# Held weight loads, and reciprocals and small layernorm terms on ScalarE, in a fused attention and gated-MLP block

## The chip, the cores and the metric

The kernel runs on one core of a Trainium2 chip. The metric is the device time in microseconds, taken as the median of several runs; the profile shows one execution. The engines are named as the profile names them: PE (TensorE, matmuls), PEld (its weight loads), DVE (VectorE), ACT (ScalarE), POOL (GpSimd) and SP (SyncE, from whose queue every DMA of this kernel is issued). L12 means line 12 of the kernel before.

## The reference

The block is linear attention followed by a gated MLP, each with a layernorm in front and a residual around it, on x of shape 1 x 2048 x 1024 in bf16:

```python
def _A_ref(x, wqkv, wo):
    B, S, D = x.shape
    H = 32; Dh = D // H
    qkv = (lambda x, *d: x.transpose(*d))((x @ wqkv).reshape(B, S, 3, H, Dh), 2, 0, 3, 1, 4)
    q, k, v = qkv[0], qkv[1], qkv[2]
    phi = lambda t: jnp.where(t > 0, t + 1, jnp.exp(t)) + 1e-6
    pq, pk = phi(q), phi(k)
    kv = jnp.einsum("bhsd,bhse->bhde", pk, v)
    z = jnp.einsum("bhsd->bhd", pk)
    num = jnp.einsum("bhqd,bhde->bhqe", pq, kv)
    den = jnp.einsum("bhqd,bhd->bhq", pq, z)[..., None] + 1e-6
    o = num / den
    return (lambda x, *d: x.transpose(*d))(o, 0, 2, 1, 3).reshape(B, S, D) @ wo

def _B_ref(x, W_gate, W_up, W_down):
    gate = jnp.einsum("bsd,df->bsf", x, W_gate)
    up = jnp.einsum("bsd,df->bsf", x, W_up)
    gate = gate * (lambda x, dt: x.astype(dt))(gate > 0, gate.dtype)
    h = gate * up
    return jnp.einsum("bsf,fd->bsd", h, W_down)

x = A_x
h = x + _A_ref(_layernorm(x, axis=-1), A_wqkv, A_wo)
h2 = h + _B_ref(_layernorm(h, axis=-1), B_W_gate, B_W_up, B_W_down)
```

F, the width of the MLP, is 3584.

## The kernel before

The large products are done with Strassen's scheme (seven products of half-size blocks in place of eight), so each needs sums of blocks of its left and right operands, which DVE makes. The 2048 tokens are 16 tiles of 128.

The work goes through these stages:

- *K and V* (0 to 124.7 us in the profile). `ln_T` loads a tile of x, normalises it and transposes it into xT. Tiles are taken in four units of four; `k_unit` and `v_unit` make K (with phi applied, tile pk, which lies in wo_mem) and V, and `kv_tile` adds up kv and z. The weight sums of Q (`q_sums`, L127 to L130 on tiles wq_sb and tq) stand at the end of this stage in the code, but run as soon as DVE's order allows. Q's weights wq_sb are loaded with two DMAs of 1 MB (L372), written in the code after unit 0.
- *Q of the first half* (124.7 to about 149 us): `q_unit(0, c)` writes phi(Q) into pqT.
- *Attention, steps 0 to 7* (to about 203 us). For each of the 16 token tiles there are five stages, begun at a lag of 0, 1, 1, 2 and 4 steps: `nd` (num and den by matmuls, L473, in three pieces of 3, 3 and 2 chunks, each in one PSUM bank; den on ACT, L477; its reciprocal on DVE, L479; the product o_sb on DVE, L480), `oT` (a transposing DMA, L487), `x_in` (a load of the residual, L491), `wo_h` (the product with wo, L500; the residual and row sums, L502; a store of h, L505; the layernorm, L510 to L516) and `hn_T` (a transposing DMA, L519). The matmuls of Q's second half, `rest`, are dealt out over these eight steps.
- *Attention, steps 8 to 19* (to 299 us). The first four feature chunks of the MLP's first token half fill PE between the steps (`begin`, `narrow`, L612). Their weights come from `load_group` of groups 0 and 1, the early loads: wg and wu, each in two halves of 512 KB (L453), eight DMAs in all, written in the code before step 0 and all issued in one go. Their sums are L559 to L562.
- *The rest of the MLP* (299 to 768.6 us): gate and up by `quad_steps`, with each further weight group loaded as it is reached, then the product with W_down (`down`).

The PSUM pool of tag "ab" has three banks. `nd` takes three of them in a step and `wo_h` two, so attn's matmuls wait until o_sb has been made out of a bank. o_sb has two buffers.

Each engine and the queue of SP run their instructions in order; the framework places the instructions by its own estimate of when each is ready, with earlier code first, and adds the waits. The tile pool of wg and wu reuses memory of the Q stage, so the early loads wait for the last phi of Q's first half (L191 on DVE, just before 153 us).

Of the kernel before, what the change touches and what calls it, by code (L numbers as in the profile page):

```python
# [7 lines left out]
ACT = mybir.ActivationFunctionType  # L8
ALU = mybir.AluOpType
# [22 lines left out]
def block_kernel(ctx: ExitStack, tc: tile.TileContext, x, wqkv, wo, wg, wu, wd, out, H: int):  # L32
    nc = tc.nc
# [87 lines left out]
    def right_ops(w, t):  # L121

        (b11, b12), (b21, b22) = [[w[:, k * KH:(k + 1) * KH, j * NW:(j + 1) * NW] for j in range(2)] for k in range(2)]
        t1, t2, t4, t3 = t[:, 0], t[:, 1], t[:, 2], b12.bitcast(FP16)

        def sums():
            nc.vector.tensor_tensor(out=t1, in0=b12, in1=b11, op=ALU.subtract)  # L127
            nc.vector.tensor_tensor(out=t2, in0=b22, in1=t1, op=ALU.subtract)
            nc.vector.tensor_tensor(out=t3, in0=b22, in1=b12, op=ALU.subtract)
            nc.vector.tensor_tensor(out=t4, in0=b21, in1=t2, op=ALU.subtract)  # L130

        return (b11, b21, b22, t4, t1, t2, t3), sums

    def strassen(pool, work, mm, fin, sbufs=3):

# [65 lines left out]
    with ExitStack() as actx:  # L201
# [16 lines left out]
        def load_w(dst, j, col):  # L218
            nc.sync.dma_start(out=dst[:, :, j * NW:(j + 1) * NW], in_=wqkv_v[:, :, col + j * NW:col + (j + 1) * NW])
# [144 lines left out]
        for n, t in enumerate(units[0]):  # L364
# [3 lines left out]
            if n == 1:  # L368
                sums_unit(1)
                k_sums()  # L370
        for j in range(2):
            load_w(wq_sb, j, 0)  # L372
        for u in range(1, NU):
            todo = atiles[4 * u + 4:4 * u + 8]
            for _ in k_unit(u):
                if todo:
                    ln_T(todo.pop(0))
            if u == 1:
                v_sums()
            for t in units[u - 1]:  # L380
                kv_tile(t)
            new_v(u)
            for n, _ in enumerate(v_unit(u)):
                if n == 1 and u + 1 < NU:
                    sums_unit(u + 1)
# [60 lines left out]
    wu_v = wu.rearrange("(kc p) (h f) -> p kc h f", p=P, h=2)  # L446

    def load_group(g):
        tiles = []
        for nm, v in (("wg", wg_v), ("wu", wu_v)):  # L450
            w_sb = wpool.tile([P, KC, 2, GP * P], BF16, tag=nm, name=nm)
            for h in range(2):
                nc.sync.dma_start(out=w_sb[:, :, h, :], in_=v[:, :, h, g * GP * P:(g + 1) * GP * P])  # L453
            tiles.append(w_sb)
        return tiles

    early = [load_group(g) for g in range(NE // GP)]
    pieces = [(c, min(GPB, KC - c)) for c in range(0, KC, GPB)]

    def attn_stages(t):  # L460

# [4 lines left out]
        def nd():  # L466
            o_sb = bwork.tile([P, D], BF16, tag="o_sb", name="o_sb")
            st["o"] = o_sb
            ov = o_sb[:].rearrange("p (k h e) -> p k h e", k=KC, h=HPC)
            for c0, n in pieces:  # L470
                ps = ndpool.tile([P, NW], FP32, tag="ab", name="nd")
                for c in range(c0, c0 + n):
                    nc.tensor.matmul(ps[:, (c - c0) * NDW:(c - c0 + 1) * NDW], lhsT=pqT[:, c, t * P:(t + 1) * P],  # L473
                                     rhs=kvz[:, c, :], start=True, stop=True)
                ndv = ps[:, 0:n * NDW].rearrange("p (k w) -> p k w", w=NDW)
                den = bsmall.tile([P, GPB, HPC], FP32, tag="den", name="den")
                nc.scalar.activation(out=den[:, 0:n], in_=ndv[:, :, P:NDW], func=ACT.Identity, bias=deps[:], scale=1.0)  # L477
                rd = bsmall.tile([P, GPB, HPC], FP32, tag="rd", name="rd")
                nc.vector.reciprocal(out=rd[:, 0:n], in_=den[:, 0:n])  # L479
                nc.vector.tensor_tensor(  # L480
                    out=ov[:, c0:c0 + n], in0=ndv[:, :, 0:P].rearrange("p k (h e) -> p k h e", h=HPC),
                    in1=rd[:, 0:n, :].unsqueeze(3).to_broadcast([P, n, HPC, Dh]), op=ALU.mult)
# [11 lines left out]
        def wo_h():  # L494
# [12 lines left out]

            sm = bsmall.tile([P, 6], FP32, tag="sm", name="sm")
            nmean, var, lnv, rstd, nmr = (sm[:, i:i + 1] for i in range(5))
            nc.vector.tensor_tensor(out=nmean, in0=tot[:, 0:1], in1=tot[:, 1:2], op=ALU.add)  # L510
            nc.vector.tensor_scalar(out=nmean, in0=nmean, scalar1=-1.0 / D, scalar2=None, op0=ALU.mult)
            nc.scalar.activation(out=st["hn"][:], in_=h_sb[:], func=ACT.Square, bias=nmean, scale=1.0, accum_out=var)
            nc.scalar.activation(out=lnv, in_=var, func=ACT.Ln, bias=LN_EPS, scale=1.0 / D)
            nc.scalar.activation(out=rstd, in_=lnv, func=ACT.Exp, scale=-0.5)
            nc.vector.tensor_tensor(out=nmr, in0=nmean, in1=rstd, op=ALU.mult)
            nc.scalar.activation(out=st["hn"][:], in_=h_sb[:], func=ACT.Identity, bias=nmr, scale=rstd)  # L516

        def hn_T():
# [19 lines left out]
    rest = [p for s in range(1, NS) for c in range(0, KH, 2) for p in [q_unit(s, c)] * 6]  # L538
    for step in range(QSTEPS):
        attn_step(step)  # L540
        for p in rest[step * len(rest) // QSTEPS:(step + 1) * len(rest) // QSTEPS]:
            next(p)
    q1ctx.close()
# [153 lines left out]
    for n, items in enumerate(todo):  # L697
# [2 lines left out]
            for q in range(4):  # L700
                nc.sync.dma_start(out=hh0[q][:, 0:NE, :], in_=hh_dram[0][q][:, 0:NE, :])
        if n >= NE:
            wt = load_group(items[0][2])
            w = {fi: sums(wt, fi) for fi in range(GP)}
        if n == len(todo) - 1:
            first_wd = load_wd(0, 0, 0, prepool)
# [163 lines left out]
```

## Time and profile before

| what | value |
|---|---|
| median of 7 runs | 772.88 us (770.54 to 775.36) |
| the profiled execution | 770.78 us |
| its span in the profile | 768.6 us |
| mean granted clock of PE | 0.998 |
| PE busy, 0 to 20 us | 11.19 us |
| PE busy, 20 to 60 us | 37.75 us of 40 |
| PE busy, 124.7 to 148.9 us | 24.09 us of 24.2 |
| PE busy, 299 to 595.1 us | 291.51 us of 296.1 |
| PE busy, 595.1 to 768.6 us | 169.07 us of 173.5 |
| early weight loads (wg, wu), issue to landing | 5.4 and 5.5 us, median of all |
| wq_sb loads, issue to landing | 11.4 us, median of two |
| oT and hn transposes, issue to landing | 3.1 and 3.5 us, median |

The page gives busy time for each engine, and the windows give the same for chosen stretches. Busy times of neighbouring instructions on one engine overlap a little. In a line of the timeline, the bracket at the end tells how long the engine had been idle before the instruction and what released it. A wait for several things is put down to the one that came last.

In the K and V stage DVE has been the fuller engine from 20 to 60 us (38.75 of 40), with the DMA engines full up to about 26 us. The four sums of Q's weights run on DVE at 64.1, 65.8, 67.0 and 69.9 us, each 1.21 us, though the first matmul that needs wq_sb starts at 124.7 us. The page's DMA part lists SP as the issuer of every transfer: 89.15 MB through one hardware queue.

### The profile page before, as it was taken

What the parts mean: (1) busy time and instruction counts of PE and PEld (TensorE: products, weight loads), DVE (VectorE), ACT (ScalarE), POOL (GpSimd) and SP (SyncE); (2) the same over time, 40 slices, a digit from 0 to 9 for tenths busy, and PEclk for the clock granted to TensorE, in tenths of its full rate; (3) what the DMA queues carried; (4) which work ended last, traced back from release to release, by engine and by line L of the source; (5) the groups of instructions that cost most, each with busy time, mean ns of one, the idle gap of its engine ahead of it and who ended that gap; (6) DMA issues with size and microseconds to landing.
All of it is one profiled execution on the core that took longest, in us unless ns stands there. A gap on an engine that the chain in (4) does not pass through costs nothing.

```text
span 768.6 us, 9558 instructions
## 1 busy us (share of the span) xinstructions
PE 736.5 (96%) x3524; PEld 339.2 (44%) x3584; DVE 488.9 (64%) x948; ACT 313.6 (41%) x529; POOL 3.8 (0%) x34
## 2 busy tenths in 40 slices
PE   5989999989889999999999999999998999999998
PEld 2444555434444444444444444444443444444443
DVE  5999454877897776656374554746545891349632
ACT  4876554866757554444444444444444000000000
POOL 0000000000000000000000000000000000000000
PEclk9999999999999999999999999999999999999999
DMA  9961003095786526154023140140001986971001
GB/s 320 255 137 41 1 1 110 1 246 137 177 173 166 135 76 195 60 158 130 7 73 86 34 130 8 41 118 28 29 7 46 332 263 205 314 270 49 28 27 55
DMA packets 125150, 89.76 MB, mean 117 GB/s; under 512 B 50352, under 2 KB 116912, under 8 KB 124592
## 3 DMA queue, kind: packets, MB, share of 16 engines
q1 hardware_dynamic: 125104, 89.15, 40.8%
q8 instruction: 28, 0.46, 0.2%
q14 instruction: 18, 0.15, 0.1%
HBM read 59.77 MB, written 17.83 MB: 101 GB/s over the span
## 4 chain that ended last, share of the span: by engine, by line
PE 49%; DVE 13%; ACT 4%; issue 3%; DMA 3%; DVEq 0%; SPq 0%; ACTq 0%
PE A L579 15%; PE accA L740 10%; PE E L579 8%; PE accE L740 6%; DVE gu L598 4%; PE Dp L579 3%; PE attn L500 2%; ACT snap L593 2%; DMA hn<-hn 2%; PE accD L740 2%; PE Aq L612 1%; DVE hh L601 1%; DMA out_dram<-o 1%; ACT gu L600 1%; DVE x_res L502 1%
## 5 line engine op out<-in xcount | busy, mean ns | idle before, releaser
L598 DVE TENSOR_TENSOR gu<-E,snap 128x1024 bf16<-128x1024 f32 x48 | 58.6, 1222 | 90.1 <-ACT snap L593 87.5
L593 ACT COPY snap<-A 128x1024 f32<-128x1024 f32 x72 | 72.1, 1008 | 84.0 <-PE A L579 84.0
L740 PEld LDWEIGHTS <-hh 128*128 128x128 bf16 (+1 forms) x560 | 54.7, 98 | 67.6 <-DVE gu L598 1.8
L600 ACT ACTIVATE gu<-gu 128x512 bf16<-128x512 bf16 x72 | 45.4, 630 | 86.2 <-DVE gu L598 85.9
L740 PE MATMUL accA<-wd,hh 128*128 128x512 f16 (+1 forms) x333 | 73.2, 379 | 1.5 <-DVE gu L598 1.3
L500 PE MATMUL attn<-wo_mem,oT 128*128 128x512 bf16 x250 | 58.8, 385 | 8.3 <-DMA oT<-o_sb 3.4
L579 PEld LDWEIGHTS <-tg 128*128 128x128 f16 x384 | 37.5, 98 | 49.5 <-issue 5.7
L579 PEld LDWEIGHTS <-tu 128*128 128x128 f16 x384 | 37.5, 98 | 45.4
L601 DVE TENSOR_TENSOR hh<-gu 128x512 bf16<-128x512 bf16 x72 | 30.4, 422 | 38.4 <-ACT gu L600 38.4
L579 PE MATMUL A<-hn,tg 128*128 128x512 f16 (+1 forms) x191 | 49.2, 379 | 1.2 <-ACT snap L593 1.1
L579 PE MATMUL A<-hn,tu 128*128 128x512 f16 (+1 forms) x192 | 49.3, 379 | 0.0
L143 ACT COPY u<-Aq 128x512 f32<-128x512 f32 x56 | 32.1, 582 | 40.4 <-PE Aq L276 20.3
L579 PEld LDWEIGHTS <-wg 128*128 128x128 bf16 x288 | 28.1, 98 | 34.5 <-issue 1.1
L579 PEld LDWEIGHTS <-wu 128*128 128x128 bf16 x288 | 28.2, 98 | 34.0
L500 PEld LDWEIGHTS <-oT 128*128 128x128 bf16 x256 | 24.4, 99 | 40.8 <-issue 10.5
L740 PEld LDWEIGHTS <-s 128*128 128x128 f16 x224 | 21.9, 98 | 27.2 <-issue 0.8
L598 DVE TENSOR_TENSOR gu<-Dp,snap 128x1024 bf16<-128x1024 f32 x24 | 29.3, 1219 | 2.3 <-PE Dp L579 2.3
L276 PEld LDWEIGHTS <-xT 128*128 128x128 bf16 (+1 forms) x192 | 18.6, 98 | 23.1 <-issue 1.5
L748 DVE TENSOR_TENSOR u<-accA,hres 128x512 f32<-128x512 f32 x16 | 10.7, 686 | 28.2 <-PE accA L740 27.6
L189 ACT ACTIVATE e<-pq_mem,negb 128x512 bf16<-128x512 bf16 x32 | 22.7, 720 | 10.6 <-DVE pq_mem L184 10.5
L502 DVE SCALAR_TENSOR_TENSOR x_res<-attn,x_res 128x512 bf16<-128x512 f32 x32 | 21.9, 686 | 7.9 <-PE attn L500 7.9
L480 DVE TENSOR_TENSOR o_sb<-nd,rd 128x384 bf16<-128x384 f32 (+1 forms) x48 | 23.1, 508 | 4.0 <-DMA oT<-o_sb 3.2
(159 smaller groups left out, 1207.2 us busy)
## 6 DMA issues: line engine op xcount, KB each, us to landing
wd<-in_B_W_down_dram SPq DMA_DIRECT2D x16, 896.0 KB, 6.9
hh_dram<-hh SPq DMA_DIRECT2D x72, 128.0 KB, 1.7
wg<-in_B_W_gate_dram SPq DMA_DIRECT2D x14, 512.0 KB, 5.4
wu<-in_B_W_up_dram SPq DMA_DIRECT2D x14, 512.0 KB, 5.5
hh<-hh_dram SPq DMA_DIRECT2D x4, 1792.0 KB, 8.3
x_sb<-in_A_x_dram SPq DMA_DIRECT2D x16, 256.0 KB, 3.8
x_res<-in_A_x_dram SPq DMA_DIRECT2D x16, 256.0 KB, 3.0
h_dram<-x_res SPq DMA_DIRECT2D x16, 256.0 KB, 2.6
```

What stands on the lines that cost most here:

```text
L143: nc.scalar.copy(out=snaps[nm, v], in_=A[v][:])
L189: nc.scalar.activation(out=e, in_=dst, func=ACT.Exp, bias=negb[:, 0:1], scale=1.0)
L276: nc.tensor.matmul(ps[:], lhsT=left[m - 1][:, kc, r + v * P:r + (v + 1) * P], rhs=right[m - 1][:, kc, :], start=(start and kc == 0), stop= ...
L480: nc.vector.tensor_tensor(out=ov[:, c0:c0 + n], in0=ndv[:, :, 0:P].rearrange("p k (h e) -> p k h e", h=HPC), in1=rd[:, 0:n, :].unsqueeze(3 ...
L500: nc.tensor.matmul(ps[:], lhsT=st["oT"][:, c, :], rhs=wo_sb[:, c, j * NW:(j + 1) * NW], start=(c == 0), stop=(c == KC - 1))
L502: nc.vector.scalar_tensor_tensor(out=h_sb[:, j * NW:(j + 1) * NW], in0=ps[:], scalar=1.0, in1=h_sb[:, j * NW:(j + 1) * NW], op0=ALU.mult, ...
L579: nc.tensor.matmul(ps[:, v, :], lhsT=w[v][m - 1][:, kc, :], rhs=left[m - 1][:, kc, :], start=(start and kc == 0), stop=(kc == KH - 1), ski ...
L593: nc.scalar.copy(out=m[:], in_=ps[:])
L598: nc.vector.tensor_tensor(out=gu[:], in0=ps[:], in1=m[:], op=ALU.add)
L600: nc.scalar.activation(out=gu[:, 0, :], in_=gu[:, 0, :], func=ACT.Relu)
L601: nc.vector.tensor_tensor(out=d, in0=gu[:, 0, :], in1=gu[:, 1, :], op=ALU.mult)
L740: nc.tensor.matmul(accs[tt][:], lhsT=lhs[:, half * FD + f, tt * P:(tt + 1) * P], rhs=rhs[half][:, f, :], start=(start and half == 0 and f ...
```

## The change

There are four edits.

1. A helper `hold(dst, src)` copies on POOL. Called with a single element of a tile that a DMA is about to fill, and a single element of a tile that some step produces, it makes the DMA wait for that step: the DMA writes over the copied element, so it comes after the copy, and the copy comes after the producer.
2. The two loads of wq_sb move from after unit 0's V to after unit 1's K (in the code behind `v_sums`), each held by an element of a pk tile of unit 1.
3. The eight early loads are no longer issued when the tiles are made. They are kept in a list and issued inside the loop of steps 0 to 7: none at step 0, two at step 1, one at each of steps 2 to 7, each held by an element of that step's o_sb. `load_group` later in the MLP issues its loads at once, as before.
4. The reciprocal of den, 1/d, is taken as exp(-ln d), both on ACT: L477 becomes Ln with the same bias, and L479, a DVE reciprocal, becomes an ACT Exp with scale -1. In the layernorm of h, the two DVE instructions for the negative mean become one with two operations, and nmr, the product of negative mean and rstd, goes from DVE to ACT.

```diff
+    def hold(dst, src):
+
+        nc.gpsimd.tensor_copy(out=dst, in_=src)
...
-        for j in range(2):
-            load_w(wq_sb, j, 0)
         for u in range(1, NU):
...
             if u == 1:
                 v_sums()
+                for j in range(2):
+                    hold(wq_sb[0:1, 0, j * NW:j * NW + 1], pk[units[u][j]][0:1, 0:1])
+                    load_w(wq_sb, j, 0)
...
     def load_group(g):
-        tiles = []
+
+        tiles, loads = [], []
         for nm, v in (("wg", wg_v), ("wu", wu_v)):
             w_sb = wpool.tile([P, KC, 2, GP * P], BF16, tag=nm, name=nm)
             for h in range(2):
-                nc.sync.dma_start(out=w_sb[:, :, h, :], in_=v[:, :, h, g * GP * P:(g + 1) * GP * P])
+                def load(after=None, w_sb=w_sb, v=v, h=h):
+                    if after is not None:
+                        hold(w_sb[0:1, 0, h, 0:1], after)
+                    nc.sync.dma_start(out=w_sb[:, :, h, :], in_=v[:, :, h, g * GP * P:(g + 1) * GP * P])
+                loads.append(load)
             tiles.append(w_sb)
-        return tiles
-
-    early = [load_group(g) for g in range(NE // GP)]
+        return tiles, loads
+
+    early, early_loads = zip(*[load_group(g) for g in range(NE // GP)])
+    early_loads = [f for loads in early_loads for f in loads]
...
+            held.append(o_sb)
...
-                nc.scalar.activation(out=den[:, 0:n], in_=ndv[:, :, P:NDW], func=ACT.Identity, bias=deps[:], scale=1.0)
+                nc.scalar.activation(out=den[:, 0:n], in_=ndv[:, :, P:NDW], func=ACT.Ln, bias=deps[:], scale=1.0)
                 rd = bsmall.tile([P, GPB, HPC], FP32, tag="rd", name="rd")
-                nc.vector.reciprocal(out=rd[:, 0:n], in_=den[:, 0:n])
+                nc.scalar.activation(out=rd[:, 0:n], in_=den[:, 0:n], func=ACT.Exp, scale=-1.0)
...
-            nc.vector.tensor_tensor(out=nmean, in0=tot[:, 0:1], in1=tot[:, 1:2], op=ALU.add)
-            nc.vector.tensor_scalar(out=nmean, in0=nmean, scalar1=-1.0 / D, scalar2=None, op0=ALU.mult)
+            nc.vector.tensor_scalar(out=nmean, in0=tot[:, 0:1], scalar1=tot[:, 1:2], scalar2=-1.0 / D,
+                                    op0=ALU.add, op1=ALU.mult)
...
-            nc.vector.tensor_tensor(out=nmr, in0=nmean, in1=rstd, op=ALU.mult)
+            nc.scalar.activation(out=nmr, in_=nmean, func=ACT.Identity, scale=rstd)
...
     for step in range(QSTEPS):
         attn_step(step)
+        if step:
+            for _ in range(-(-len(early_loads) // (QSTEPS - step))):
+                early_loads.pop(0)(held[step][0:1, 0:1])
...
-            wt = load_group(items[0][2])
+            wt, loads = load_group(items[0][2])
+            for f in loads:
+                f()
```

## The prediction

> **What bounds the kernel now.** I read the page first, then the windows of the stretches that the diff touches, then PE's waits there, then the timelines of SP, PE, DVE and ACT around each wait.
>
> ```profile
> PE 736.5 (96%) x3524; PEld 339.2 (44%) x3584; DVE 488.9 (64%) x948; ACT 313.6 (41%) x529; POOL 3.8 (0%) x34
> ...
> PE   5989999989889999999999999999998999999998
> ```
>
> PE is busy for 736.5 of 768.6 us and the change takes no matmul away. So it can win only PE's idle time and time in which PE's clock is low, and can lose wherever it makes PE wait. The dips that concern it are slices 9, 11 and 12 (154 to 231 us). The windows put numbers on them (columns: window, its length, then busy time of PE, PEld, DVE, ACT, POOL; granted clock, DMA share, GB/s):
>
> ```profile
> 20.00:60.00 40.00, 37.75 (x201) 18.16 (x203) 38.75 (x86) 31.30 (x62) 0.80 (x4) 1.00 0.77 181
> 60.00:124.70 64.70, 63.90 (x360) 32.00 (x366) 38.55 (x62) 35.10 (x51) 1.12 (x7) 1.00 0.06 13
> ...
> 148.90:203.40 54.50, 50.64 (x267) 23.69 (x272) 41.63 (x136) 38.09 (x84) 0.00 (x0) 0.97 0.75 175
> 203.40:299.00 95.60, 88.37 (x442) 41.20 (x449) 78.06 (x238) 56.29 (x119) 0.00 (x0) 1.00 0.60 146
> ```
>
> PE idles 3.9 us in the first attention stretch (steps 0 to 7) and 7.2 us in the second. The first is nearly one wait. The SP timeline, then PE's, show how it comes about:
>
> ```profile
> 153.02 1.01 SPq L453 DMA_DIRECT2D wg<-in_B_W_gate_dram  x2
> 154.07 2.91 SPq L453 DMA_DIRECT2D wu<-in_B_W_up_dram  x2
> 157.02 3.52 SPq L453 DMA_DIRECT2D wg<-in_B_W_gate_dram  x2
> 160.58 3.73 SPq L453 DMA_DIRECT2D wu<-in_B_W_up_dram  x2
> 164.42 9.35 SPq L487 DMA_TRANSPOSE oT<-o_sb  x3
> ```
>
> ```profile
> 167.99 0.38 PE L409 MATMUL Eq<-xS,tq 128*128 128x512 f16 x1
> 171.81 4.91 PE L500 MATMUL attn<-wo_mem,oT 128*128 128x512 bf16 x15 [3.45 <-DMA oT<-o_sb]
> ```
>
> The eight early weight loads (512 KB each, 4.2 MB) occupy SP from 153.0 to 164.3. Step 0's o_sb was complete at about 155.0 on DVE, so its transpose is issued 9.4 us late and stands behind the 4 MB in the queue too. PE uses up its Q work and waits 3.45 us. It then starts at a granted clock of 0.66 (window 170 to 175): 16 matmuls of L500 take 3.61 us in every later step, this group 4.91, so another 1.30 us.
>
> The second stretch has no such wait. It is DVE that is full there:
>
> ```profile
> 203.40:212.40 9.00, 7.00 (x38) 3.25 (x37) 8.78 (x29) 5.30 (x12) 0.00 (x0) 1.00 0.74 158
> 212.40:218.00 5.60, 4.91 (x28) 2.43 (x28) 5.43 (x20) 3.49 (x8) 0.00 (x0) 1.00 0.73 153
> ```
>
> DVE is at 98% and 97%, ACT at 59% and 62%, and attn waits 1.81, 0.64, 0.68 and 0.68 us, step after step, on rd (L479) and o_sb (L480) of DVE.
>
> **The change, part by part.**
>
> *wq held.* Two 1 MB loads move from 13.2 us to the end of unit 1's K tiles, when L191 has run, about 60 us. What they leave: DMA is at a share of 1.1 until 26 us, but DVE, 5.00 of 5.00 busy from 20 to 25, sets that stretch, and the next x tile's load, at 27.97, waits for a buffer. Gain nothing. Where they go: SP has transposes of xT until 65.25; those behind the held loads are unit 3's, first multiplied at 96.60; then SP is empty to 124.95. Landing took 11.4 us in a full queue, so 71 us at the latest. The readers are the four q_sums on DVE (64.1 to 71.1, 1.21 us each), and wq_sb's first matmul at 124.7. From 80 to 124 DVE is busy for 22.38 of 44 us, which hides them if they come later. Behind the hold on POOL stand the v_sb memsets (56.7 to 58.2), first read by kv matmuls at 82.65. Value 0; bounds -0.5 (PE's idle time of 60 to 65, were DVE freed there) and +4.8 (q_sums ahead of their data in DVE's queue, 4 x 1.21).
>
> *Early loads held.* Two at step 1, one at each of steps 2 to 7, each behind a one-element copy on POOL that reads that step's o_sb. No POOL copy is in the trace: the nearest rows are memsets of 0.10 to 0.12 us (bounds 0.1 to 0.6, the two that took 0.59). POOL has nothing else there; an o_sb buffer is written again two steps, some 10 us, later. SP now reaches the first transpose at 155 rather than 164.4. Left out of the sum is what the last loads risk: step 7's is issued at about 200, lands 5.5 us later, and group 1's first sums run at 245.3; group 0, complete at step 3, is read at 204.9. New cost: each load takes SP 0.4 to 2 us and, at the burst's 290 GB/s, the DMA engines 1.8 us, ahead of that step's transpose. Behind a load that waits on SP stand that step's oT, x_res and hn transfers; but it waits for o_sb's first third, oT for the whole. The room: step 3's oT was issued at 180.07, lands in 3.1, and is used at 189.20, 6.0 us spare. Bounds: -4.75 (3.45 + 1.30) and 0 (the wait reappears). I take -4.2: 0.55, a third of one load's 1.8, stays in the first step, where two loads meet two transposes.
>
> *Reciprocal as Ln and Exp, and the small terms.* ACT's L477 keeps its place with another function. L479 (48 times, 0.22 us, of which about 0.14 before the next may start) leaves DVE; so do one of L510/L511 (0.135) and L515 (0.15). DVE per step: 3 x 0.14 + 0.29 = 0.7 us less. ACT per step: 3 Exp and 1 Identity. Neither form is in the trace; nearest are L514's Exp of one element (0.20) and L477 with a bias pointer (0.265). I take 0.21 and 0.20, so 0.83 us a step (bounds 0.8 and 1.1). Both functions are used throughout already, with one table load at 0.73 us, so no switch.
>
> The gain on the path, from step 9: den (first half) starts at 212.81, rd at 213.47 because x_res (L502) holds DVE till then, o_sb at 213.86, attn at 214.57. On ACT, two Ln end at 213.26 and Exp at about 213.5: o_sb starts 0.36 earlier. I take 0.3 for each of steps 8 to 15: -2.4. Bounds: -4.0 (60% of the 6.7 us that PE idles from 203.4 to 267.2) and 0.
>
> The Trainium skill ("ScalarE: Activation LUTs", sections What it computes and Rules for kernel authors) speaks against this part: it keeps reciprocals and plain multiplies on VectorE. The DVE and ACT rows of 203.4 to 218 answer that the fuller engine sets the pace here. By its figure for an ACTIVATE without pointers (What ACT_TABLE_LOAD costs), 186 ns plus 0.833 ns an element, which the 0.20 of L514 bears out, the 48 Exp are an estimated 9.4 us; all of it on the path, with -4.2 for the loads, would give 776.0.
>
> *What ACT's extra work costs in steps 2 to 7.* There ACT is fuller, since phi of Q runs on it: 3.78 + 4.73 + 5.06 + 4.38 = 17.95 of 21.5 us in the four windows of 181.9 to 203.4. With 4 x 0.83 it is 21.3: 99%. But busy times of neighbours overlap by about 0.1 (L516 takes 1.24 and the next starts after 1.13), two hops between engines go (DVE's L511 and L515 kept ACT waiting 0.3 to 0.5 each), and Q work now spreads from 157 us on instead of piling up before 168. Value +0.8; bounds 0 and +5.0 (0.83 x 6 steps).
>
> Sum: 0 - 4.2 - 2.4 + 0.8 = -5.8 us. The profiled execution took 770.78 us (span 768.6 and 2.2 around it), so 765.0. The median of 7 runs, 772.88, lies 2.1 above it: **767.1, said as 767**.
>
> **Rivals.** *ACT becomes the bound (slower).* For: the 99%. Exp sits in ACT's order behind L512 and L516 (1.14 and 1.24 us), so o_sb, and with it the bank that attn needs, comes later: half of 1.2 in each of 8 late steps is 4.8. Against: ACT is at 62% there. Price: -4.2 + 5.0 + 4.8 = +5.6, so 776.4 and 778.5 as a median; milder forms lie from 772 up. It decides once ACT is over 95% busy in steps 2 to 7. Chance 0.17.
>
> *The stall is only spread (no change).* DMA shares in steps 4 to 7 are 0.83, 0.68, 0.94 and 0.72; a load adds 1.8/5.4 = 0.33, which makes 1.0 to 1.27, and the burst itself showed 1.15 to 1.23. If each of seven steps lasts 0.7 longer, +4.9 eats the 4.2: 770.78 - 4.2 + 4.9 - 2.4 = 769.1, median 771.2. Against: 6.0 us spare for each oT. Chance 0.12.
>
> *The wq hold holds nothing useful and stalls DVE.* The 4.8 of above: 765.0 + 4.8 = 769.8, median 771.9. For: the sums sat in a full stretch at 64 us. Against: half of DVE's time is free after 80. Chance 0.05.
>
> **How the numbers follow.** The forecast has 0.66; its own range is 763 (-4.75 - 4.0 - 0.5 = -9.3 gives 763.6) to 770.5. Telling a change from none takes 0.3%, 2.3 us: below 770.6 is faster, above 775.2 slower. The two middle rivals are "same" (0.17), the ACT rival slower (0.17), the forecast faster (0.66). For 8 in 10 the range goes on through the middle rivals to 774.5.
>
> **What would show it.** Right: the first oT is issued near 155, attn starts before 162, no PE gap over 2 us and a clock of 1.00 from 150 to 205; weight loads one by one between transposes on SP; PE idle from there to the end of the attention steps down from 7.2 to about 5; DVE under 95% and ACT near 75% in steps 8 and 9. Wrong: attn or nd waiting for ACT's rd, ACT snaps of Q late (PE waiting for L143), oT landing in over 6 us at every step, DVE idle before tq. The forecast fails if PE's gaps in steps 2 to 7 add up to more than the 4.75 us they replace.

## The result, and the profile after

| what | before | after |
|---|---|---|
| median of all runs | 772.88 us (47 runs) | 769.69 us (20 runs) |
| the profiled execution | 770.78 us | 769.0 us |
| its span | 768.6 us | 767.2 us |
| its mean granted clock of PE | 0.998 | 1.000 |
| mean granted clock of the runs that list it | 0.996 (101 runs beside the experiments) | 0.999 (21 runs) |

The changed kernel is faster by 0.4%: 0.9958 of the time before, with a 95% interval of 0.9946 to 0.9969. The forecast was 767 (763 to 774.5). The direction and the range held; the gain was 3.2 us where 5.9 was forecast.

The same stage borders as before, read as the first matmul of each stage, place the difference between the two profiled executions. The columns add up to the spans.

| stage | before | after | difference |
|---|---|---|---|
| K and V, until Q's first matmul | 124.70 | 125.15 | +0.45 |
| Q of the first half | 24.18 | 24.17 | -0.01 |
| attention, steps 0 to 7 | 54.71 | 50.95 | -3.76 |
| attention, steps 8 to 19 | 95.41 | 96.83 | +1.42 |
| gate and up | 296.13 | 296.21 | +0.08 |
| down | 173.47 | 173.89 | +0.42 |

So one stage gained about what was said, and the next one, which was to gain 2.4 us, lost 1.4. First the page of the changed kernel: busy time by engine, and PE's row of the 40 slices.

```profile
PE 735.4 (96%) x3524; PEld 339.5 (44%) x3584; DVE 481.7 (63%) x868; ACT 321.8 (42%) x593; POOL 5.9 (1%) x44
...
PE   5999999999889989999999999999998999999997
```

DVE lost 80 instructions and 7.2 us, ACT won 64 and 8.2 us, POOL the ten one-element copies: the change does what its diff says. Slice 9 (the stall) is full now; slices 11 and 12 (the second stretch) are still at 8. The windows of the changed kernel, with the columns as before, at its own stage borders:

```profile
60.00:125.15 65.15, 63.61 (x359) 31.72 (x363) 38.01 (x61) 34.46 (x50) 2.01 (x9) 1.00 0.17 45
149.32:200.27 50.95, 49.49 (x267) 23.94 (x272) 38.46 (x99) 40.87 (x113) 1.50 (x8) 1.00 0.81 188
200.30:297.10 96.80, 88.39 (x442) 41.30 (x449) 74.20 (x195) 61.82 (x155) 0.00 (x0) 1.00 0.60 144
```

PE's idle time in steps 0 to 7 went from 3.86 to 1.46 us, and the clock is 1.00. In steps 8 to 19 DVE is busy for 3.9 us less and ACT for 5.5 us more, but PE idles 8.4 us instead of 7.2.

The SP timeline of the changed kernel shows the first part at work:

```profile
155.09 1.23 SPq L501 DMA_TRANSPOSE oT<-o_sb  x1
156.41 1.22 SPq L462 DMA_DIRECT2D wg<-in_B_W_gate_dram  x2
157.76 3.00 SPq L501 DMA_TRANSPOSE oT<-o_sb  x1
160.86 0.53 SPq L462 DMA_DIRECT2D wu<-in_B_W_up_dram  x1
```

The first transpose goes out at 155.09, where it went out at 164.42 before, and the weight loads come one or two at a time between the transposes. PE's timeline of the changed kernel, at the first attn and at the two places where it waits longest:

```profile
159.38 3.61 PE L514 MATMUL attn<-wo_mem,oT 128*128 128x512 bf16 x15
...
205.23 0.23 PE L487 MATMUL nd<-kvz,pq_mem 128*128 128x132 bf16 x1 [1.79 <-DVE pq_mem L195]
206.36 3.61 PE L514 MATMUL attn<-wo_mem,oT 128*128 128x512 bf16 x16 [0.90 <-DVE o_sb L494]
...
272.36 1.02 PE L629 MATMUL Aq<-hs,tu 128*128 128x512 f16 x4 [1.50 <-ACT m L147]
```

The first attn starts at 159.38 (171.81 before), with no wait, and its 16 matmuls take 3.61 us, the length of a full clock (4.91 before). The other two places are new: 2.69 us at the border of the two stretches (2.00 before, as 0.19 and 1.81), and 1.50 us at 272, where before had no wait at all.

### The profile page after: what moved, and what is told of

Same layout as the page of the kernel before. It is cut to its first block, busy times and chain, and to the rows that moved or that the text cites. A ratio compares the mean times of both kernels' runs of the same rounds, so it can differ in the third digit from the quotient of the medians.

```text
span 767.2 us, 9550 instructions
## 1 busy us (share of the span) xinstructions
PE 735.4 (96%) x3524; PEld 339.5 (44%) x3584; DVE 481.7 (63%) x868; ACT 321.8 (42%) x593; POOL 5.9 (1%) x44
## 4 chain that ended last, share of the span: by engine, by line
PE 64%; DVE 18%; ACT 8%; DMA 6%; issue 3%; SPq 0%; DVEq 0%; ACTq 0%
PE A L596 16%; PE accA L759 10%; PE E L596 8%; PE accE L759 6%; PE attn L514 4%; PE Aq L280 4%; DVE gu L615 4%; PE Dp L596 3%; PE Aq L414 2%; DMA hn<-hn 2%; PE Eq L280 2%; PE Aq L629 2%; ACT snap L610 2%; DVE stats L249 2%; PE accD L759 2%
## 5 line engine op out<-in xcount | busy, mean ns | idle before, releaser
L147 ACT COPY u<-Aq 128x512 f32<-128x512 f32 x56 | 32.3, 582 | 44.6 <-PE Aq L280 21.0
L596 PE MATMUL E<-hs,tg 128*128 128x512 f16 x96 | 24.6, 378 | 0.9
```

Source lines behind the costliest of these rows:

```text
L147: nc.scalar.copy(out=snaps[nm, v], in_=A[v][:])
L596: nc.tensor.matmul(ps[:, v, :], lhsT=w[v][m - 1][:, kc, :], rhs=left[m - 1][:, kc, :], start=(start and kc == 0), stop=(kc == KH - 1), ski ...
```

## The experiments

The line numbers in a profile are those of its own kernel, so they differ by a few from one to the next. Before was run again beside each batch of experiments; its medians there were 772.6 to 773.0, so the ratio tells more than the difference of medians. "Clock" is the mean over a kernel's runs of PE's mean granted clock.

| kernel | median, us | ratio (95%) | clock | steps 0 to 7 | steps 8 to 19 |
|---|---|---|---|---|---|
| before | 772.88 | | 0.9959 | 54.71 | 95.41 |
| after | 769.69 | 0.9958 (0.9946 to 0.9969) | 0.9988 | 50.95 | 96.83 |
| e1: early loads alone | 769.60 | 0.9956 (0.9939 to 0.9973) | 0.9967 | 50.37 | 97.71 |
| e2: ACT edits alone | 772.10 | 0.9992 (0.9973 to 1.0011) | 0.9978 | 54.92 | 94.29 |
| e3: wq held, alone | 775.57 | 1.0042 (1.0023 to 1.0061) | 0.9936 | 56.57 | 97.24 |
| e4: all but the wq hold | 769.35 | 0.9948 (0.9933 to 0.9964) | 0.9988 | 50.95 | 96.69 |
| e11: loads and reciprocal | 770.07 | 0.9971 (0.9956 to 0.9986) | 0.9967 | 50.59 | 98.40 |
| e7: all but the reciprocal | 770.63 | 0.9969 (0.9951 to 0.9986) | 0.9976 | 51.03 | 98.55 |
| e10: loads placed, not held | 769.46 | 0.9964 (0.9947 to 0.9981) | 0.9978 | 51.40 | 95.99 |
| e12: e10 and the ACT edits | 768.63 | 0.9957 (0.9940 to 0.9975) | 0.9990 | 51.77 | 97.75 |
| e5: Q dealt over steps 0 to 6 | 772.35 | 0.9988 (0.9969 to 1.0006) | 0.9978 | 49.69 | 98.99 |
| e8: Q dealt over steps 0 to 5 | 779.43 | 1.0072 (1.0046 to 1.0098) | 0.9938 | 53.54 | 106.19 |
| e9: e4, half of the early sums on POOL | 780.65 | 1.0105 (1.0084 to 1.0126) | 0.9910 | 50.94 | 110.22 |
| e6: before, with 16 matmuls more | 775.36 | 1.0027 (1.0009 to 1.0044) | 0.9975 | 58.30 | 95.79 |

Each stage length is of one execution and contains what its clock cost in it. In e1, e3, e7, e11 and e12 the attn group at the start of step 8 takes 5.30 us in place of 3.61, so 1.7 us of their steps 8 to 19 are a halved clock. Without it, e1 stands at 96.0, e10 at 95.99, e12 at 96.1, e4 at 96.7, e11 at 96.7 and e7 at 96.9. The "1.0 us" that the expectation of e7 gives to the ACT edits there, 97.7 of e1 against 96.7 of e4, is this lost clock and not the edits.

Where K and V end, too, differs from run to run by more than the +0.45 of the table above: the nine kernels that load wq_sb as before begin Q at 123.58 to 125.66 us, the five that hold it at 124.94 to 125.87.

### The parts alone

**e1, the early loads alone.** wq_sb is loaded where before has it, and edit 4 is undone; of that, the reciprocal is shown, against the changed kernel:

```diff
...
-                nc.scalar.activation(out=den[:, 0:n], in_=ndv[:, :, P:NDW], func=ACT.Ln, bias=deps[:], scale=1.0)
+                nc.scalar.activation(out=den[:, 0:n], in_=ndv[:, :, P:NDW], func=ACT.Identity, bias=deps[:], scale=1.0)
...
-                nc.scalar.activation(out=rd[:, 0:n], in_=den[:, 0:n], func=ACT.Exp, scale=-1.0)
+                nc.vector.reciprocal(out=rd[:, 0:n], in_=den[:, 0:n])
...
```

> Only the eight early weight loads are held (edit 3); wq_sb is loaded as before, reciprocal and small terms stay on DVE. Theory A (the loads give the whole gain, 3.8 us in steps 0 to 7, and cost nothing later): ratio 0.995, 769.1 us; Q's matmuls end about 200 us, first oT issued near 155. Rival B (spreading Q's work to the end of step 7 exposes its phi to nd of step 8, which gives back 0.7 to 1.8 us): 770 to 771 us, with a PE gap of over 1 us before nd of step 8 that DVE's last phi (L191) ends.

The median is 769.60: the whole measured gain comes with this part. Steps 0 to 7 shrink by 4.34 us, where the forecast had -4.2 for this edit. But steps 8 to 19 are 2.30 longer, 97.71, and PE's timeline and the windows of e1 show why:

```profile
204.19 0.23 PE L486 MATMUL nd<-kvz,pq_mem 128*128 128x132 bf16 x1 [0.85 <-DVE pq_mem L195]
206.52 3.02 PE L513 MATMUL attn<-wo_mem,oT 128*128 128x512 bf16 x7 [2.10 <-DVE o_sb L493]
```

```profile
206.00:208.00 2.00, 1.48 (x4) 0.58 (x5) 2.00 (x7) 0.00 (x0) 0.00 (x0) 0.67 1.00 219
208.00:210.00 2.00, 2.00 (x6) 0.76 (x5) 0.24 (x1) 0.00 (x0) 0.00 (x0) 0.50 1.25 159
```

At the border of the two stretches PE waits 2.95 us in two pieces, and this execution's clock then falls to 0.50. So the stall that left step 0 has a smaller sibling at step 8. (The rows show the first seven of the 16 matmuls.) The 2.30 are 0.95 of wait (before has 2.00 there) and 1.7 of clock, less 0.35 elsewhere.

**e2, the ACT edits alone**: the diff's edit 4 in the kernel before, nothing else.

```diff
...
-                nc.vector.reciprocal(out=rd[:, 0:n], in_=den[:, 0:n])
+                nc.scalar.activation(out=rd[:, 0:n], in_=den[:, 0:n], func=ACT.Exp, scale=-1.0)
...
-            nc.vector.tensor_tensor(out=nmr, in0=nmean, in1=rstd, op=ALU.mult)
+            nc.scalar.activation(out=nmr, in_=nmean, func=ACT.Identity, scale=rstd)
```

> Only the reciprocal as Ln and Exp and the two small terms on ScalarE (edit 4); loads as before. The prediction's term for it was -2.4 in steps 8 to 15 and +0.8 in steps 2 to 7: 771.3 us. Theory A (the waits only change their place): 772.5 to 773.5 us, steps 8 to 19 not shorter than 95.4. Rival B (each late step wins 0.1 to 0.2): 771.5 to 772, steps 8 to 19 about 94.

The interval takes in no change. Steps 8 to 19 are 1.12 us shorter in its profile, less than half of the 2.4 forecast, and steps 0 to 7 are 0.21 longer. Beside the held loads the same edits win nothing in steps 8 to 19 (96.7 in e4 against 96.0 in e1 without the lost clock). Its three runs at a mean clock of 1.000 have a median of 769.23; the three of before at 1.000 have 769.53. Alone, this part is worth little.

**e3, the wq hold alone**, in the kernel before:

```diff
-        for j in range(2):
-            load_w(wq_sb, j, 0)
...
             if u == 1:
                 v_sums()
+                for j in range(2):
+                    hold(wq_sb[0:1, 0, j * NW:j * NW + 1], pk[units[u][j]][0:1, 0:1])
+                    load_w(wq_sb, j, 0)
```

> Only the two wq_sb loads held behind unit 1's K (edit 2). Theory A and B: no difference, 772.9 us. Rival C (the 0.45 us by which the changed kernel begins Q later comes from this edit, as DVE waits for wq_sb before tq): 773.3 us, the first matmul with wq_sb at 125.1 rather than 124.7.

This part by itself makes the kernel slower, by 0.4%. It keeps the stall of step 0, now 3.91 us instead of 3.45, and waits 1.81 us at step 8 like before. In before the second wait did not cost the clock; in e3's profile both did, the first at twice before's price (3.4 us lost from 170 to 180, where before lost 1.7 from 170 to 176). PE's timeline and the windows of e3:

```profile
173.28 3.15 PE L505 MATMUL attn<-wo_mem,oT 128*128 128x512 bf16 x7 [3.91 <-DMA oT<-o_sb]
...
211.84 2.58 PE L505 MATMUL attn<-wo_mem,oT 128*128 128x512 bf16 x8 [1.81 <-DVE rd L484]
```

```profile
174.00:176.00 2.00, 2.00 (x6) 0.73 (x5) 0.57 (x1) 0.72 (x1) 0.00 (x0) 0.50 0.77 74
...
214.00:216.00 2.00, 2.00 (x6) 0.68 (x5) 1.54 (x5) 0.42 (x1) 0.00 (x0) 0.50 1.09 251
```

Nine of its 12 runs have a mean clock of 0.993, where before has 23 of 101. By the line through before's runs (below, 0.62 us for 0.001) its lower clock, 0.9936 against 0.9959, is an estimated 1.4 of the 2.6 us. Why its wait at step 0 is 0.46 us longer is not settled. What the hold does at its own place is seen in DVE's timeline of the changed kernel:

```profile
70.51 1.22 DVE L127 TENSOR_TENSOR tq<-wq_sb 128x2048 f16<-128x2048 bf16 x1 [2.46 <-DMA wq_sb<-in_A_wqkv_dram]
```

The first q_sum stands ahead of its data in DVE's queue for 2.46 us, with copies of V behind it; PE then waits 0.92 us at 75.32. That is the third rival's mechanism: DVE loses about half of the 4.8 us it was given there, PE 0.92.

**e4, all but the wq hold**: the changed kernel with the wq loads back after unit 0.

```diff
+        for j in range(2):
+            load_w(wq_sb, j, 0)
...
-                for j in range(2):
-                    hold(wq_sb[0:1, 0, j * NW:j * NW + 1], pk[units[u][j]][0:1, 0:1])
-                    load_w(wq_sb, j, 0)
```

> Edits 3 and 4 without the wq_sb hold (edit 2). If C holds, 0.4 us faster than the changed kernel: 769.3. If edit 2 does nothing, 769.7. Steps 8 to 19: with rival B, a gap of over 1 us before nd of step 8 and 96 to 97 us in all; if the gap of 1.5 us at the ACT copy of the last chunk comes from the order of ACT alone and by chance, it may be absent here.

769.35, against 769.69 with the hold: not told apart. Runs at a mean clock of 1.000 point the same way (767.9 in five runs, 768.8 in nine of the changed kernel), but the runs are few, and Q's first matmul, at 125.01 here and 125.15 there, says nothing, given the spread of that border. The hold may cost up to 1 us beside the other edits and has brought nothing in any run.

### The two halves of the ACT edits

**e11** is e1 with the reciprocal on ACT, the small layernorm terms left on DVE (first diff, against e1); **e7** is the changed kernel with the reciprocal back on DVE (second diff, against the changed kernel). In both, the function of den goes with it, Ln or Identity.

```diff
...
-                nc.vector.reciprocal(out=rd[:, 0:n], in_=den[:, 0:n])
+                nc.scalar.activation(out=rd[:, 0:n], in_=den[:, 0:n], func=ACT.Exp, scale=-1.0)
```

> Loads held and the reciprocal on ScalarE; the small layernorm terms on DVE as before, wq_sb as before. If the reciprocal alone makes the gain of the ScalarE edits in steps 8 to 19, 96.7 there and 769.4 us. If the small terms are needed for it: 97.2 to 97.7 and 769.9. The gap of 1.5 us at the ACT copy at about 272 is absent if the small terms cause it.

```diff
...
-                nc.scalar.activation(out=rd[:, 0:n], in_=den[:, 0:n], func=ACT.Exp, scale=-1.0)
+                nc.vector.reciprocal(out=rd[:, 0:n], in_=den[:, 0:n])
```

> The changed kernel with the reciprocal back on DVE (den by Identity on ScalarE); the small layernorm terms stay on ScalarE. If the reciprocal makes the 1.0 us that the ScalarE edits win in steps 8 to 19: 97.5 there, 770.3 us. If the small terms make it: 96.7, 769.7 us. Steps 0 to 7: 50.4 rather than 50.95 if ScalarE's fuller queue was what cost 0.58 there.

770.07 and 770.63: neither half beside the loads is better than the loads alone (769.60), and both expectations for steps 8 to 19 built on a gain that was e1's lost clock. What the halves do differ in is the new wait at 272 us. It is there in every kernel with the small layernorm edits (0.83 us in e7, 0.99 in e12, 1.07 in e2, 1.49 in e4, 1.50 after, and in e5, e8 and e9) and in none without (before, e1, e3, e6, e10, e11). ACT's timeline of the changed kernel shows how it arises:

```profile
270.59 1.15 ACT L526 ACTIVATE hn<-x_res,sm 128x1024 bf16<-128x1024 bf16 x1 [1.70 <-DVE sm L524]
...
271.74 0.57 ACT L147 COPY m<-Aq 128x512 f32<-128x512 f32 x1
```

L526, a pass of the layernorm, waits 1.70 us for DVE's merged L524; behind it in ACT's order stands the copy L147, which frees a PSUM bank, and PE needs the bank. ACT's order was the same before, but there L512 waited only 0.20. What is new lies on DVE, in the changed kernel's timeline:

```profile
268.73 0.42 DVE L111 TENSOR_TENSOR hs<-hn 128x512 f16<-128x512 bf16 x1 [0.87 <-DMA hn<-hn]
...
269.40 0.68 DVE L516 SCALAR_TENSOR_TENSOR x_res<-attn,x_res 128x512 bf16<-128x512 f32 x1
...
270.35 0.21 DVE L524 TENSOR_SCALAR sm<-tot 128x1 f32<-128x1 f32 x1
```

The sum L111, which waits 0.87 us for hn's transpose, now stands ahead of x_res and of the mean in DVE's order. Before, it came after both, so it did not hold them up:

```profile
272.36 0.15 DVE L511 TENSOR_SCALAR sm<-sm 128x1 f32<-128x1 f32 x1
272.79 0.43 DVE L111 TENSOR_TENSOR hs<-hn 128x512 f16<-128x512 bf16 x1 [0.27 <-DMA hn<-hn]
```

Which of the two small edits (the merged mean or nmr on ACT) brings this order was not tried.

### Held, or only placed?

**e10** is e1 with the loads at the same places in the code but without the one-element copy; **e12** is e10 with the ACT edits.

```diff
-                early_loads.pop(0)(held[step][0:1, 0:1])
+                early_loads.pop(0)()
```

> Loads alone, issued at the same places in the loop of steps 0 to 7 but without the one-element copy. If the place in the code is enough, as the run with loads held alone: 769.6, oT first issued by 156. If the copy is what matters, SP takes the loads as soon as their memory is free: two before the first transposes and the rest in pairs between them; then the first oT is late by two loads (some 3 us of SP and queue), PE waits up to 3 us there, and the time lies at 770.5 to 772.

> The loads at their places in the loop without the one-element copy, and the ScalarE edits; wq_sb as before. If the parts add as they did with the copy (loads with ScalarE edits 769.35, loads held alone 769.6, loads placed alone 769.46): 769.2 us, not to be told from the changed kernel's 769.69; steps 0 to 7 at 51 to 52 us with a wait of 1 us at the first attn. If the copy matters once ScalarE carries more: 770 or more.

769.46 and 768.63, level with 769.60 and 769.35 of their held twins. The place in the code does nearly all of it, as SP's timeline of e10 shows:

```profile
153.98 1.00 SPq L461 DMA_DIRECT2D wg<-in_B_W_gate_dram  x2
155.55 4.04 SPq L500 DMA_TRANSPOSE oT<-o_sb  x2
159.65 1.19 SPq L461 DMA_DIRECT2D wu<-in_B_W_up_dram  x2
```

Two loads now go ahead of the first transpose, not eight, and it leaves at 155.55, 0.46 us later than with the copies. PE waits 1.01 us before the first attn, where the held form (e1) has none; the bracket puts it down to a copy on ACT, but the first transpose, too, lands later, at 160.7 in place of 158.7:

```profile
161.49 3.61 PE L513 MATMUL attn<-wo_mem,oT 128*128 128x512 bf16 x16 [1.01 <-ACT u L147]
```

The profile of e10 is shorter than e1's all the same (766.8 against 768.1 us): its wait of 2.84 us at step 8 did not cost the clock, and e1's 2.95 did.

### Steps 8 to 19

**e5 and e8** ask whether the late wait at 205 comes from the end of Q's matmuls. They deal `rest` over seven and six steps instead of eight:

```diff
-        for p in rest[step * len(rest) // QSTEPS:(step + 1) * len(rest) // QSTEPS]:
+        for p in rest[step * len(rest) // (QSTEPS - 1):(step + 1) * len(rest) // (QSTEPS - 1)]:
```

> The changed kernel with Q's second half dealt over steps 0 to 6 rather than 0 to 7, nothing left out. Theory B (holding the loads lets Q's matmuls run to the end of step 7, so that nd of step 8 waits for their phi, 1.79 and 0.90 us): that gap goes, steps 8 to 19 fall from 96.8 to about 95, 768 us. Rival (the step-8 gap comes from DVE's weight sums, which are there in any order): the gap stays at over 1.5 us in all and the time at 769.7.

```diff
-        for p in rest[step * len(rest) // QSTEPS:(step + 1) * len(rest) // QSTEPS]:
+        for p in rest[step * len(rest) // (QSTEPS - 2):(step + 1) * len(rest) // (QSTEPS - 2)]:
```

> As the run with Q dealt over steps 0 to 6, but over 0 to 5. Theory B: the gap before nd of step 8 is gone here too, but steps 6 and 7 have no Q work to cover nd's evacuation, so that attn waits there as it does in steps 8 to 12 (0.65 each): 768 to 769.5 us. Rival: 769.7 or more.

The wait of nd for the last phi of Q goes, but the time does not: e5's steps 8 to 19 are 98.99 us where about 95 were expected, its median is 772.35, and e8, expected at 768 to 769.5, is slower than before. In e8 PE waits 4.20 us for o_sb at the attn of 197.06, where no Q work is left to fill the step. In PE's timeline of e5 a wait has come up one place earlier:

```profile
199.73 1.86 PE L629 MATMUL Aq<-hn,wg 128*128 128x512 bf16 x4 [2.37 <-ACT sm L528]
```

The bracket names an ACT instruction of the next tile, whose result this product does not read. What it does read is the fourth tile's hn: ACT ended it at 193.42, its transpose was issued on SP at 196.06, behind an oT, and landed 3.6 us later, at 199.6. So in e5 moving Q's matmuls does not free anything: with Q finished earlier, PE reaches the MLP's first product before hn is there. The explanation by Q's tail alone falls.

**e9** takes work off DVE at the place where it is fullest. It is e4 with the sums of wu for the four early chunks on POOL:

```diff
-        return [weight_sums(wt[0], fi, "tg"), weight_sums(wt[1], fi, "tu")]
+        return [weight_sums(wt[0], fi, "tg"), weight_sums(wt[1], fi, "tu", eng)]
...
-            st["q"] = quad_steps(0, f, sums(early[f // GP], f % GP), None)()
+            st["q"] = quad_steps(0, f, sums(early[f // GP], f % GP, nc.gpsimd), None)()
```

> Loads held and ScalarE edits, without the wq_sb hold, and in addition the four sums of wu for the four early chunks on POOL instead of DVE (4 of 0.42 us a chunk). If DVE's order around step 8 sets the late steps (weight sums, phi of Q and o_sb queue there), 1 to 1.7 us faster: 768. Rival (POOL is far slower at it, and the second matmuls of each product wait for tu, or POOL and DVE slow each other): 770 or more.

It lost 11 us against e4. POOL's timeline of e9, then DVE's, then DVE's of e4 for the same kind of sum:

```profile
204.55 1.33 POOL L578 TENSOR_TENSOR tu<-wu,tu 128x512 f16<-128x512 bf16 x1
205.84 1.33 POOL L576 TENSOR_TENSOR tu<-wu,tu 128x512 f16<-128x512 bf16 x1
207.13 1.33 POOL L577 TENSOR_TENSOR tu<-wu 128x512 f16<-128x512 bf16 x1
```

```profile
202.20 0.68 DVE L188 SCALAR_TENSOR_TENSOR pq_mem<-Eq,u 128x512 bf16<-128x512 f32 x1
...
203.50 1.37 DVE L577 TENSOR_TENSOR tg<-wg 128x512 f16<-128x512 bf16 x1
204.79 1.37 DVE L576 TENSOR_TENSOR tg<-wg,tg 128x512 f16<-128x512 bf16 x1
```

```profile
202.73 0.42 DVE L577 TENSOR_TENSOR tg<-wg 128x512 f16<-128x512 bf16 x1
```

While POOL runs its sums of 1.33 us, one every 1.29, DVE's sums take 1.37 in place of 0.42 (the first of them 0.77), one every 1.29 too: the two engines alternate. The phi step L188, which reads PSUM, keeps its 0.68. At 210.62 PE has waited 7.19 us for DVE. So this run says nothing on what an emptier DVE would bring; it says that POOL, at 1.15 us at the least for such a sum, can't be used for it.

### The clock

**e6** was to keep PE busy through the stall of step 0 and so to part the lost clock from the wait. It adds to the kernel before 16 matmuls whose product is not read:

```diff
+            if t == order[0]:
+                junk = pspool.tile([P, NW], FP32, tag="D", bufs=1, name="junk")
+                for c in range(16):
+                    nc.tensor.matmul(junk[:], lhsT=wo_sb[:, c % KC, 0:P], rhs=wo_sb[:, c % KC, 0:NW],
+                                     start=True, stop=True)
```

> The kernel before with 16 matmuls more, on wo's weights into an unused bank ahead of the first attn matmuls, whose result nobody reads: they fill the 3.45 us in which PE waits for the first oT, and shorten nothing. Clock theory (about 2 of the 3.2 us of the change are PE's granted clock, which falls to 0.50 for some 3.4 us after a wait of this length): wait and first attn stay at 171.8, attn then takes 3.61 and not 4.91 us, the mean clock of the runs rises from about 0.996 to 0.998 or more, and the median falls by 1.3 to 2, to 771. Rival (the spread between runs has another cause, DMA or the start): 772.9 or slower.

It missed its aim. The matmuls were placed before the last of Q's, from 157.15 us on, not in the gap, and PE's timeline of e6 has the wait and the slow matmuls of before:

```profile
171.08 4.99 PE L505 MATMUL attn<-wo_mem,oT 128*128 128x512 bf16 x16 [3.19 <-DVE o_sb L480]
```

The 775.36 falls under the expectation's rival, but neither theory was put to the test. The run leaves open what the wait costs at a full clock. e2 answers that by chance: its profile has the same wait, 3.51 us, and no loss of clock. The same two microseconds after that wait, in the windows of before and of e2:

```profile
172.00:174.00 2.00, 2.00 (x6) 0.68 (x5) 1.10 (x3) 0.72 (x1) 0.00 (x0) 0.50 0.17 39
```

```profile
172.00:174.00 2.00, 2.00 (x9) 0.94 (x11) 1.37 (x4) 0.70 (x1) 0.00 (x0) 1.00 0.08 18
```

So much the same wait costs the clock in one execution and not in another. The two kernels differ by the ACT edits, but the runs of before alone spread too, from a mean clock of 0.993 to 1.000. All of those in the batches, sorted by it, show what this is worth:

| mean clock of the run | runs of before | their median, us | runs after | their median, us |
|---|---|---|---|---|
| 0.999 to 1.000 | 3 | 769.53 | 13 | 769.00 |
| 0.997 to 0.998 | 36 | 770.94 | 7 | 770.18 |
| 0.995 to 0.996 | 39 | 773.04 | 1 | 771.78 |
| 0.993 | 23 | 774.29 | 0 | |

A straight line through the 101 runs of before gives 770.1 at a clock of 1.000 and 0.62 us for each 0.001 below it; the same for the 21 runs of the changed kernel gives 768.8. The means are 772.7 and 769.5. So of the 3.2 us between the means, an estimated 1.9 are clock (2.5 lost before, 0.7 after), and 1.3 are left at equal clock; by the runs at 0.999 and above alone, only three of them before's, it is 0.5. The clock accounts for about half of the spread of each kernel (46% of the variance of before, 50% after); within one row of the table before's runs still differ by up to 4 us, and what does that is not shown.

## Why the prediction was right, and where not

**The early loads: right.** Forecast -4.2 us, measured -4.34 alone in steps 0 to 7. Every sign named for it came: the first transpose near 155 (155.09), attn before 162 (159.38), no gap over 2 us and a clock of 1.00 from 150 to 205, loads one by one. The transposes got slower, as feared (oT's median of 5.0 us from issue to landing from 149 to 200, 3.2 in before's same steps), and the spare time given for them, 6.0 us, covered it. The early loads themselves land sooner: wg in 4.9 and wu in 4.4 us, where before the eight took 6.4 and 7.3 (the 5.4 and 5.5 of the first table are medians of all loads of wg and wu). That the stall would only be spread is thereby out.

**ACT's extra work in steps 2 to 7: right in size.** Forecast +0.8, measured +0.58 (50.95 in e4 against 50.37 in e1; +0.37 in e12 against e10). The size is right; that ACT's fuller queue causes it is not shown: e11, with the reciprocal alone on ACT, has 50.59, and e7, with the reciprocal back on DVE, has 51.03 where its expectation said 50.4. The instructions came out at 0.207 us (Exp, 0.21 said) and 0.294 (Identity with a pointer for scale, 0.20 said). The 99% did not come: ACT was busy for 17.61 of the last 21.77 us before 200.27, 81%. The forecast's 99% counted four attention steps into that stretch, as before had (in 181.9 to 203.4 us: four of each layernorm pass, 12 of den, 5 of phi's L189). After, the steps begin earlier, in the time that had been the stall, and the stretch holds three: three of each pass, 7 of den and 7 of L193, phi's. So the rival in which ACT becomes the bound is out.

**The reciprocal on ACT in steps 8 to 15: wrong, and the step that failed.** The forecast was 0.3 us for each of eight steps, because o_sb "starts 0.36 earlier". It had 0.36 from two Ln and one Exp on ACT against the reciprocal on DVE, and took for granted that DVE would go to o_sb as soon as rd was there. DVE's timeline of step 9, first of before, then of the changed kernel:

```profile
212.86 0.68 DVE L502 SCALAR_TENSOR_TENSOR x_res<-attn,x_res 128x512 bf16<-128x512 f32 x1
...
213.67 0.22 DVE L479 RECIPROCAL rd<-den 128x12 f32<-128x12 f32 x1
213.80 0.13 DVE L511 TENSOR_SCALAR sm<-sm 128x1 f32<-128x1 f32 x1
213.86 1.02 DVE L480 TENSOR_TENSOR o_sb<-nd,rd 128x384 bf16<-128x384 f32 x2
```

```profile
210.23 0.68 DVE L516 SCALAR_TENSOR_TENSOR x_res<-attn,x_res 128x512 bf16<-128x512 f32 x1
...
210.84 0.42 DVE L112 TENSOR_TENSOR hs<-hs,hn 128x512 f16<-128x512 f16 x1
211.17 0.21 DVE L524 TENSOR_SCALAR sm<-tot 128x1 f32<-128x1 f32 x1
211.30 1.01 DVE L494 TENSOR_TENSOR o_sb<-nd,rd 128x384 bf16<-128x384 f32 x2
```

In the changed kernel the two Exp on ACT have ended at 210.87. But between x_res and o_sb, where the reciprocals stood, DVE now runs a sum of hn (L112) and the merged mean, and o_sb starts 1.11 us after den's start at 210.19; before it was 1.05, from 212.81. Attn follows den by 1.71 us, before by 1.76. The freed place was filled by other work in DVE's fixed order, so the time was saved on DVE and not on the path. PE's waits for o_sb at the attn of steps 9, 10 and 11 tell the same: 0.64, 0.68 and 0.68 us before, 0.65, 0.39 and 0.65 after. And from 232 us on before's PE waits for o_sb at most 0.40 us in a step, so eight equal gains of 0.3 were not there to be had. The sign named for this step says the same: DVE was to fall under 95% in steps 8 and 9, and is at 9.52 of 9.70 and 5.51 of 5.60 us, 98% in both (ACT is at 67% and 72%, near the 75% named). Over the eight intervals from the first attn of the stretch on, the changed kernel is 0.84 us shorter (57.43 against 58.27 us from the seventh start of attn to the fifteenth), 0.1 a step in place of 0.3.

**What ate the rest: two longer waits that the forecast did not have.** PE's waits from 149 to 298 us in the changed kernel (columns: sum, times, longest):

```profile
PE attn L514 <- DVE o_sb L494: 3.4, 7, 0.9
PE nd L487 <- DVE pq_mem L195: 2.2, 2, 1.8
PE Aq L629 <- ACT m L147: 1.5, 1, 1.5
PE nd L487 <- DVE x_res L516: 1.3, 1, 1.3
```

The first is at 205: from the first product of the MLP to the next attn it is 0.70 us longer than before (6.09 against 5.39). Not the end of Q is new: before, too, its last matmul stands right ahead of the MLP's first product (203.37 and 203.59; after, 199.84 and 200.27), and its last phi among the eight weight sums of the first chunk. But DVE is done with that phi 4.7 us after Q's last matmul, where before it was 3.1, with an earlier piece of phi (L194 and L195, from 201.27) ahead of it in DVE's order. PE's waits at this border add up to 2.69 to 2.95 us in all seven kernels that move the loads, deal Q over eight steps and leave the sums on DVE, and to 1.76 to 2.00 in before, e2 and e3. That links the longer wait to the moved loads, but e6, which does not move them, has 2.73, and e5 and e8 did not separate the causes. So the cause of the 0.70 stays open. The second is the 1.50 us at 272 behind ACT's L526, in an interval between two attn that is 1.50 longer (12.02 against 10.52). The rest of the stage is 0.06 longer. So +0.70 - 0.84 + 1.50 + 0.06 makes the +1.42; of the 3.8 us between it and the forecast of -2.4, 1.6 are the gain per step that did not come and 2.2 the two waits. The sign named for this stretch, PE's idle time down from 7.2 to about 5, failed with it: it is 8.4.

**wq held: 0 was said, a small loss is likelier.** The loads landed in 5.1 to 6.8 us, and the first sum waited for them until 70.51 (71 was given as the latest). The bound of 4.8 was not reached; 0.3 to 1 us beside the other edits, not resolved, and 2.6 alone, of which an estimated 1.4 is clock.

**From the profiled execution to the median: a wrong step that helped.** The forecast added 2.1 us, by which before's median lies above its profiled execution. The table of clocks says what this was: the profiled execution had lost clock once (0.998), the median run about twice (0.996). That is not an addition that any kernel carries; it is lost in the waits, and the change removes the longest of them. After it the same difference is 0.7. The sum's own figure, 765.0, missed the 769.0 of the profiled execution by 4.0; with the offset the miss is 2.7, since two errors of opposite sign met. That was luck: with 0.7 for the offset the forecast's own range would have ended at 769.1, short of the 769.69.

**Not accounted for:** the 0.42 us in the down stage. The last store lands 1.7 us after its issue in both, but then the span goes on for 1.37 us, before for 0.90, until the program's last drains are through. The late one is POOL's, which itself takes 0.21 us in place of 0.08. The seven kernels whose last work on POOL is a one-element copy have 1.29 to 1.40 us there, the seven others 0.89 to 0.90; e9, which has the copies and sums on POOL after them, is among these. Why a copy on POOL 570 us earlier should lengthen the end is not shown. (e3's down stage is as long, 174.24 us, with the short end; that is open too.)

The Trainium skill ("TensorE: Matmul & The Clock Gate", Part 1: The HAM clock gate) has PE at half speed after at least one idle window of about 3.4 us, with windows that run freely; from this it would follow that the price of a gap depends on where it falls. The halved clock, its length (before's windows from 170 to 176 lose 1.7 us, 3.4 us at half speed) and e2 against before agree. Its rule to avoid gaps of more than about 3 us (Why this matters for your kernels) is too mild for this kernel: 2.95 us in two pieces (e1) and 1.81 us in one (e3), neither of which holds a whole such window, were followed by a clock of 0.50 as well, and the measurement decides.

## What to carry to other kernels

When a queue that runs in order holds a burst of loads that are not needed soon, ahead of a small transfer that is, deal the loads out over the steps; the place in the code did nearly all of it here, and the forced hold added little. Work taken from a full engine shortens the path only if the engine's next instruction is the one that is waited for: read what the order will put into the freed place before counting the time. And before adding the difference between a profiled execution and the median to a forecast, ask what it consists of: here most of it was clock lost behind waits, and the change removed one of them.

## What the runs showed of the hardware that was not expected

- About half of the spread between runs of one kernel is here clock: the medians of before's runs go from 769.5 us at a mean of 1.000 to 774.3 at 0.993, in three steps of 1.2 to 2.1 us, near the 1.7 that one stretch of 3.4 us at 0.50 costs.
- Much the same wait halves the clock in one execution and not in another (3.45 us in before did, 3.51 in e2 did not; 1.83 and 0.90 in e12 did, 1.79 and 0.90 after did not), and 1.81 us was enough once (e3).
- A tensor_tensor on POOL with both inputs in SBUF (128x512, bf16 to f16) takes 1.15 to 1.36 us where DVE's takes 0.42, and while such instructions run, DVE's bf16 sums take up to 1.37. The Trainium skill ("SBUF — State Buffer", SBUF: two separate sides) describes a pair of ports that the two engines share as an exclusive lock for a whole instruction; the alternation in e9, one instruction of each in 1.29 us, agrees with it, and so does the 0.68 of the DVE instruction that reads PSUM.
